# First feed-forward product by the 448 queries of a batch, in a fused attention and feed-forward kernel

## The chip, the core and the metric

The kernel runs on one core of a Trainium2 chip. The metric is the device time of one execution in microseconds (us); lower is better. The core has five engines that run their own instruction streams side by side: TensorE (PE, matmuls; its weight loads are listed apart as PEld), VectorE (DVE), ScalarE (ACT), GpSimd (POOL) and SyncE (SP, which here only issues DMA transfers). Matmul results go to PSUM, which has eight banks of 128 partitions x 512 fp32 values; everything else on the chip lives in SBUF.

## The reference

Attention over 8 batches, 8 heads, 576 positions, head size 64, with a block-causal mask of 64 positions, followed by a feed-forward network over all 4,608 tokens. The weights of the network come in fp64.

```python
scores = (1 / 8) * q @ k.T                       # per batch and head
mask = (pos[:, None] // 64) >= (pos[None, :] // 64)
attn = softmax(where(mask, scores, -1e9))
x = (attn @ v).transpose(0, 2, 1, 3).reshape(4608, 512)
h = x @ w_in                                     # 512 -> 2048
g = h / (1 + exp(-h))
out = g @ w_out                                  # 2048 -> 512
```

## The kernel before, in words

**Precision.** A product that must be near fp32 is made of three matmuls of reduced fp32 (fp32r): each factor is split into a rounded part (`hi`) and the rest (`lo`), and hi*hi, hi*lo and lo*hi are summed in PSUM. ScalarE makes the `hi` copies, GpSimd or VectorE the `lo` differences.

**Attention.** The queries 0 to 127 of every batch (the blocks 0 and 1 of 64) see few keys and are done first, by themselves: the names `a` and `b` in the order table are two groups for queries 0 to 63, `c0` to `c3` four groups for queries 64 to 127. What they give is four blocks of 256 tokens of `x` (blocks 0 to 3). The other 448 queries of a batch and head are one unit, `u0` to `u63`: a batch takes eight units, two heads (a pair of units) fill one of the four 128-row chunks of `x`. A unit has ten score matmuls on TensorE (L639; query widths 448, 320, 192, 448 and 64, each once with the hi and once with the lo part of the queries), then VectorE works on the scores in PSUM: maxima (L582), their spreading over rows (L586), and the subtraction of the maximum (`sub`, L682, L685, and L676 for the half-masked squares). ScalarE takes the exponent (L692), GpSimd splits queries and keys and adds the exponents up (L621, L625, L698, L701). For a pair of units follow twenty matmuls with the values (L742), one multiplication by the inverse sums on VectorE (L746), the `hi` copy of the new chunk of `x` on ScalarE (`x_hi`, L763) and the `lo` difference on GpSimd (`x_lo`, L767).

**First product.** The 3,584 tokens of the units are packed into blocks of 256, numbered 4 to 17, whatever their batch. `ffn1(blk, d, f)` (L970 to L981) makes 128 rows of `h` for one block: four chunks of the contraction by three passes, twelve matmuls 128x256 (L981). Two calls (f = 0 and 1) fill one PSUM bank, of which there are two; ScalarE copies it to SBUF (`keep`, L988) and a DMA takes it to a scratch tensor in HBM (`save`). There are 18 x 16 = 288 such calls. A chunk of `x` of one block is one of 16 tiles, which are given out from a free list as blocks fill and come free when a block's last call is made; a pair's 448 queries fall in two or three blocks (`pieces`, L748 to L759), so `x_hi` and `x_lo` are two or three instructions.

**Weights.** The pieces of `w_in`, `w0` to `w15`, are loaded at the start (L443), turned from fp64 into fp32 (`rebias`, `sign`, `bits`), and split. `w_out` follows as `o0` to `o15` (L447; `rebias` L458). Its eight pairs become the factors `t0` to `t7`: sums of quarters on GpSimd (`x`, L556, L558, L560), `hi` on ScalarE (L570) and `lo` on GpSimd (L575), four parts each, numbered 0 to 3.

**Second product.** `i0` to `i71` are items: a quarter of the contraction for one block, read back from HBM, put through silu (L1006), combined and split, and multiplied in seven products instead of eight (L1055). `y0` to `y17` gather the output. The factors t0 to t7 must all be there soon after the first item starts.

**What sets the order.** Nothing on the chip or in a compiler sorts the work: `ORDER` (L62 to L380) is a table of tokens, and each token emits its instructions on the engines that they run on, so every engine's stream stands in the order of the table. `ffn`, `keep` and `save` take the next call off a queue; the calls of the first product are laid between the steps of the attention so that TensorE has work while the other engines prepare the next unit. `warm:N` puts N small matmuls on zeros there (L783) where TensorE has nothing else. The last 43 calls of `ffn` stand after the last unit and ahead of the first matmul of the second product (`i0.prod:0`); t3 to t7 are made beside them.

Of the kernel before, what the change touches and what calls it, by code (L numbers as in the profile page):

```python
# [66 lines left out]
c0.max:0 w1.hi b.turn:1 c0.exp:0 w2.bits:0 w1.lo warm:8 c0.scores:1 w2.bits:2 w9.load w5.rebias b.back:0 ffn w10.load b.back:1
c0.max:1 w2.hi c1.load c0.exp:1 w2.lo b.pv w3.rebias c0.sum ffn all.mask o0.load w7.rebias w3.bits:0 c3.load_v c0.norm b.hi:0
w3.bits:2 b.hi:1 keep b.lo:0 w11.load w3.hi b.lo:1 warm:8 c0.turn:0 w6.rebias w3.lo w4.bits:0 save c3.scores:0 c0.back:0 w4.bits:1
c0.turn:1 o1.rebias w8.rebias c3.max:0 ffn w4.bits:2 c0.back:1 c3.exp:0 w12.load w5.bits:0 c0.pv w5.bits:1 w4.hi c3.scores:1  # L70
c1.load_v c0.hi w5.bits:2 w4.lo ffn c0.lo w13.load w5.hi c3.max:1 o0.rebias w5.lo w9.rebias w6.bits:0 c1.scores:0 c3.exp:1
w6.bits:1 ffn c1.max:0 keep c3.sum c1.exp:0 w6.bits:2 save c3.norm warm:5 c1.scores:1 w14.load w7.bits:0 w6.hi w7.bits:1
w10.rebias w6.lo c3.turn:0 w7.bits:2 c2.load ffn c1.max:1 c3.back:0 w15.load w8.bits:0 c1.exp:1 c3.turn:1 w8.bits:1 ffn c3.back:1
c1.sum w8.bits:2 w7.hi c1.norm keep warm:8 c1.turn:0 w9.bits:0 w8.hi save w9.bits:1 w11.rebias w7.lo w9.bits:2 c3.pv c1.back:0
w10.bits:0 w8.lo w9.hi c1.turn:1 w10.bits:1 w12.rebias ffn c1.back:1 w9.lo w10.bits:2 w13.rebias w11.bits:0 c1.pv keep w11.bits:1
w10.hi save ffn c1.hi c2.load_v w11.bits:2 w10.lo w14.rebias c1.lo w11.hi c2.scores:0 w12.bits:0 w15.rebias w11.lo w12.bits:1 ffn
u0.load c2.max:0 w12.bits:2 c2.exp:0 warm:5 c2.scores:1 w13.bits:0 w12.hi w13.bits:1 keep w12.lo ffn w13.bits:2 save c2.max:1
w13.hi u1.load w14.bits:0 c2.exp:1 w13.lo ffn w14.bits:1 u0.split_hi c2.sum ffn w14.bits:2 c2.norm keep w15.bits:0 w14.hi save
warm:3 c2.turn:0 w15.bits:1 u0.split_k w15.bits:2 ffn c2.back:0 o0.bits:0 w15.hi u0.split_q o0.bits:1 c2.turn:1 keep ffn o0.bits:2
w14.lo c2.back:1 u2.load o1.bits:0 save c2.pv w15.lo all.staged o1.bits:1 o2.load u0.load_v o1.bits:2 ffn c2.hi u2.load_v t0.x:0  # L80
c3.hi u3.load_v c2.lo t0.hi:0 u1.load_v c3.lo u0.scores t0.hi:1 o3.load t0.lo:0 keep u0.max:0 t0.hi:2 t0.lo:1 save u0.max:1 ffn
u1.split_hi u0.max:2 t0.lo:2 ffn u0.gather u1.split_q u0.top u0.spread ffn keep u0.wide u1.split_k save u0.sub:0 ffn u0.sub:2
u0.exp:0 u3.load t0.x:1 u0.sub:1 u0.exp:2 u1.scores t0.x:2 keep u1.max:0 u0.add:0 u0.exp:1 save u1.max:1 o2.rebias ffn u0.add:1
u2.split_hi u1.max:2 ffn u0.sums:0 u1.gather u2.split_q u0.sums:1 o3.rebias u1.top o2.bits:0 ffn u1.spread u2.split_k o2.bits:1
keep u1.wide t0.hi:3 ffn save o2.bits:2 u4.load t0.lo:3 u1.sub:0 t1.hi:0 ffn o4.load u1.sub:2 u1.exp:0 t1.lo:0 keep u1.sub:1
u1.exp:2 save o3.bits:0 u2.scores u1.exp:1 u1.add:0 u2.max:0 u2.max:1 u1.pv u3.split_hi u1.add:1 u2.max:2 u3.split_k u1.sums:0
u2.gather u1.sums:1 u2.top ffn u1.sums_x u4.load_v u2.spread o3.bits:1 u3.split_q u5.load_v u1.sums_g u2.wide ffn o3.bits:2
u1.sums_m u5.load keep u2.sub:0 t1.hi:1 u2.sub:2 save u2.exp:0 ffn o5.load u2.sub:1 u2.exp:2 t1.lo:1 u1.inverse u2.exp:1 u3.scores
keep u2.add:0 u2.sums:0 u3.max:0 save ffn u3.max:1 u2.add:1 u4.split_hi u1.mult t1.x:0 u2.sums:1 ffn u1.x_hi u3.max:2 u1.x_lo
t1.hi:2 ffn u3.gather keep u3.top u4.split_q u3.spread ffn save u3.wide u4.split_k ffn u3.sub:0 keep u3.sub:1 u6.load t1.x:1  # L90
u3.exp:0 u3.sub:2 u3.exp:1 u4.scores t1.x:2 save u3.exp:2 u4.max:0 t1.lo:2 o5.rebias u4.max:1 u3.pv u5.split_hi u3.sums:0 u3.add:0
u4.max:2 o4.rebias u3.add:1 u4.gather o4.bits:0 ffn u6.load_v t1.hi:3 u5.split_k u3.sums:1 u7.load_v u4.top u3.sums_x u4.spread
o4.bits:1 ffn u5.split_q u3.sums_g u4.wide o4.bits:2 keep u3.sums_m ffn u7.load u4.sub:0 t2.hi:0 u4.sub:2 u4.exp:0 save u4.sub:1
u5.scores u4.exp:2 t1.lo:3 keep u5.max:0 u4.exp:1 u5.max:1 save ffn u6.split_hi u4.add:0 u5.max:2 ffn u6.split_k u4.sums:0
u5.gather u3.inverse u5.top ffn u3.mult u6.split_q u5.spread o5.bits:0 u3.x_hi u5.wide u3.x_lo u8.load ffn keep o5.bits:1 save
u5.sub:0 u4.add:1 ffn u5.sub:2 u5.exp:0 t2.lo:0 keep u4.sums:1 u5.exp:2 u5.sub:1 u6.scores save u5.add:0 u6.max:0 u5.exp:1
u6.max:1 u5.pv u7.split_hi u5.add:1 u6.max:2 u7.split_q u5.sums:0 u6.gather u5.sums:1 u6.top ffn u5.sums_x u7.split_k u8.load_v
u6.spread o5.bits:2 u9.load_v u5.sums_g u6.wide ffn t2.hi:1 u9.load u5.sums_m u6.sub:0 keep u6.sub:2 u6.exp:0 save u6.sub:1
u7.scores u6.exp:2 t2.x:0 u7.max:0 u6.exp:1 u7.max:1 ffn u8.split_hi u6.add:0 u6.sums:0 u7.max:2 t2.hi:2 ffn u6.add:1 keep
u5.inverse u7.gather save u8.split_q u6.sums:1 ffn u5.mult u8.split_k u7.top u7.spread ffn u5.x_hi u7.wide u10.load u5.x_lo keep  # L100
u7.sub:0 ffn u7.sub:2 u7.exp:0 save t2.x:1 u7.sub:1 u7.exp:2 u8.scores t2.x:2 keep u8.max:0 u7.exp:1 save u7.add:0 u8.max:1
t2.hi:3 u7.pv u9.split_hi u8.max:2 u7.add:1 u7.sums:0 u9.split_q u8.gather u7.sums:1 u8.top ffn u7.sums_x u10.load_v u8.spread
u9.split_k u11.load_v u7.sums_g u8.wide ffn u8.sub:0 u11.load u7.sums_m u8.sub:2 u8.exp:0 u8.sub:1 u9.scores u8.exp:2 keep
u9.max:0 u8.add:0 u8.exp:1 u7.inverse save ffn u10.split_hi u8.add:1 u9.max:1 ffn u7.mult u10.split_q u9.max:2 u7.x_hi u7.x_lo ffn
u8.sums:0 u9.gather u8.sums:1 keep u9.top u10.split_k ffn u9.spread save u9.wide u12.load t2.lo:2 ffn u9.sub:0 keep u9.sub:2
u9.exp:0 save t2.lo:1 u9.sub:1 u9.exp:2 u10.scores u9.exp:1 u10.max:0 u9.add:0 u10.max:1 u9.pv u11.split_hi u10.max:2 u9.add:1
u9.sums:0 u11.split_q u10.gather u9.sums:1 u10.top ffn u9.sums_x u12.load_v u10.spread u11.split_k u13.load_v u9.sums_g u10.wide
ffn u10.sub:0 keep u13.load u9.sums_m u10.sub:2 u10.exp:0 save u10.sub:1 u11.scores u10.exp:2 u11.max:0 u10.exp:1 u10.add:0
u11.max:1 ffn u12.split_hi u10.add:1 u11.max:2 ffn u12.split_q u10.sums:0 u11.gather u10.sums:1 keep u9.inverse u12.split_k ffn
save u11.top u9.mult u11.spread u9.x_hi u14.load ffn t2.lo:3 u11.wide keep u11.sub:0 u9.x_lo u11.sub:2 save u11.exp:0 ffn  # L110
u11.sub:1 u11.exp:2 u11.add:0 u11.exp:1 u12.scores keep u12.max:0 u11.add:1 save u12.max:1 u11.pv u13.split_hi u12.max:2
u13.split_q u11.sums:0 u12.gather u11.sums:1 u12.top ffn u11.sums_x u13.split_k u14.load_v u12.spread u15.load_v u11.sums_g
u12.wide ffn u15.load u11.sums_m u12.sub:0 u12.sub:2 u12.exp:0 u12.sub:1 u13.scores u12.exp:2 keep u13.max:0 u12.add:0 u12.exp:1
u13.max:1 save ffn u14.split_hi u12.add:1 u13.max:2 ffn u14.split_q u12.sums:0 u13.gather u12.sums:1 u11.inverse u14.split_k ffn
# [1086 lines left out]
```

## Time and profile before

| what | value |
|---|---|
| median of three executions | 1017.56 us (1017.47 to 1017.73) |
| the profiled execution, its own time | 1016.87 us |
| span of that execution in the trace | 1014.8 us |
| mean granted clock of TensorE | 0.999 of full speed |
| early queries and weights, up to the first score matmul of u0 | 0 to 71.45 us |
| units, with the first product between them | 71.45 to 583.4 us |
| rest of the first product, factors t3 to t7 | 583.4 to 645.4 us |
| second product | 645.4 to 1014.8 us |

The profile is that of one execution. Its own time is 2.07 us more than the span between its first and its last instruction. A row of a grouped view reads: line, engine, operation, output <- input, shape, how many; busy time and mean duration of one; idle time of the engine just before, and whose work ended it. Matmuls overlap in TensorE, so their durations (285 ns on the mean at L981) are longer than the distance between two starts; that distance comes from runs of many equal matmuls in the timeline.

### The profile page before, as it was taken

What the parts mean: (1) busy time and instruction counts of PE and PEld (TensorE: products, weight loads), DVE (VectorE), ACT (ScalarE), POOL (GpSimd) and SP (SyncE); (2) the same over time, 40 slices, a digit from 0 to 9 for tenths busy, and PEclk for the clock granted to TensorE, in tenths of its full rate; (3) what the DMA queues carried; (4) which work ended last, traced back from release to release, by engine and by line L of the source; (5) the groups of instructions that cost most, each with busy time, mean ns of one, the idle gap of its engine ahead of it and who ended that gap; (6) DMA issues with size and microseconds to landing.
All of it is one profiled execution on the core that took longest, in us unless ns stands there. A gap on an engine that the chain in (4) does not pass through costs nothing.

```text
span 1014.8 us, 23816 instructions
## 1 busy us (share of the span) xinstructions
PE 1003.3 (99%) x8532; PEld 946.3 (93%) x8532; DVE 763.0 (75%) x1969; ACT 695.8 (69%) x1587; POOL 626.9 (62%) x770
## 2 busy tenths in 40 slices
...
GB/s 355 362 184 199 138 152 156 151 133 145 149 148 148 141 151 150 150 139 144 149 157 143 74 180 198 205 177 136 146 125 125 141 131 130 131 136 130 141 43 42
DMA packets 76535, 155.70 MB, mean 153 GB/s; under 512 B 9344, under 2 KB 17536, under 8 KB 76416
## 3 DMA queue, kind: packets, MB, share of 16 engines
...
## 4 chain that ended last, share of the span: by engine, by line
PE 92%; ACT 3%; DVE 2%; DMA 2%; issue 1%; POOL 1%; SPq 0%; DVEq 0%; POOLq 0%; ACTq 0%
PE h L981 40%; PE S L1055 24%; PE c L1055 10%; PE S L639 9%; PE U L742 8%; DMA wst<-in_moe_w_in_dram 2%; ACT MR L936 1%; PE S L925 1%; PE S L811 0%; DVE h L1026 0%; ACT x L1039 0%; POOL MR L804 0%; PE S L956 0%; DVE S L1026 0%; ACT wi L1039 0%
## 5 line engine op out<-in xcount | busy, mean ns | idle before, releaser
L981 PE MATMUL h<-x,wi 128*128 128x256 f32 x3456 | 434.7, 285 | 0.6 <-ACT x L763 0.5
L981 PEld LDWEIGHTS h<-x,wi 128*128 128x128 f32 x3456 | 418.9, 191 | 4.2 <-issue 0.9
L582 DVE TRANSPOSE_TENSOR_REDUCE Mx<-S 64x4 f32<-64x128 f32 (+4 forms) x384 | 130.3, 401 | 39.3 <-PE S L639 39.3
L692 ACT ACTIVATE p<-T 128x512 f32<-128x512 f32 (+1 forms) x192 | 112.7, 611 | 27.6 <-DVE T L682 22.1
L988 ACT COPY g<-h 128x512 f32<-128x512 f32 x144 | 84.0, 583 | 41.9 <-PE h L981 31.6
L1043 POOL TENSOR_TENSOR wi<-raw,wi 128x512 fp32r<-128x512 f32 (+1 forms) x56 | 56.9, 1017 | 77.7 <-ACT wi L1039 65.8
L1043 POOL TENSOR_TENSOR x<-raw,x 128x512 fp32r<-128x512 f32 (+1 forms) x58 | 58.9, 1017 | 74.1 <-ACT x L1039 60.0
L617 ACT CAST qh<-qk 128x1024 fp32r<-128x1024 f32 x64 | 67.0, 1048 | 46.8 <-POOL pa L698 21.4
L621 POOL TENSOR_TENSOR qh<-qk,qh 64x576 fp32r<-64x576 f32 x64 | 91.5, 1429 | 6.6 <-POOL pa L698 0.9
L625 POOL TENSOR_TENSOR ql<-qk,qh 128x448 fp32r<-128x448 f32 x64 | 73.7, 1151 | 34.0 <-ACT qh L617 31.8
L698 POOL TENSOR_TENSOR pa<-p 128x448 f32<-128x448 f32 x64 | 73.8, 1153 | 33.6 <-ACT p L692 32.3
L639 PE MATMUL S<-qh 128*128 128x448 f32 (+3 forms) x320 | 91.8, 300 | 0.0
L1006 ACT ACTIVATE raw<-raw 128x1024 f32<-128x1024 f32 x72 | 76.4, 1061 | 19.8 <-DMA raw<-gd 19.4
L742 PE MATMUL U<-p,v 128*64 128x448 f32 (+3 forms) x640 | 86.5, 417 | 0.0
L639 PE MATMUL S<-ql,qh 128*128 128x448 f32 (+3 forms) x320 | 83.6, 306 | 0.0
L742 PEld LDWEIGHTS U<-p,v 128*64 128x64 f32 x640 | 43.0, 137 | 40.5 <-issue 29.8
L685 DVE TENSOR_TENSOR T<-S,MR 128x384 f32<-128x384 f32 (+2 forms) x192 | 73.5, 407 | 0.0
L639 PEld LDWEIGHTS S<-ql,qh 128*128 128x128 f32 (+1 forms) x320 | 57.0, 178 | 5.2
L586 DVE STREAM_TRANSPOSE MR<-m 128x448 f32<-128x448 f32 x64 | 41.3, 645 | 26.9 <-ACT m L664 26.9
L701 POOL TENSOR_TENSOR pa<-pa,p 128x320 f32<-128x320 f32 x64 | 56.1, 876 | 5.3 <-POOL pa L698 0.3
L639 PEld LDWEIGHTS S<-qh 128*128 128x128 f32 (+1 forms) x320 | 57.2, 179 | 2.0
L1043 POOL TENSOR_TENSOR gc<-raw,gc 128x512 fp32r<-128x512 f32 (+1 forms) x30 | 30.5, 1018 | 44.4 <-ACT gc L1039 41.3
...
## 6 DMA issues: line engine op xcount, KB each, us to landing
gd<-g SPq DMA_DIRECT2D x144, 256.0 KB, 2.7
raw<-gd SPq DMA_DIRECT2D x144, 256.0 KB, 2.9
qk<-in_qk_dram SPq DMA_DIRECT2D x128, 256.0 KB, 3.8
...
```

The source lines that it names most:

```text
L582: nc.vector.tensor_reduce(out=out, in_=in_, axis=AX.X, op=op, apply_transpose=True)
L621: nc.gpsimd.tensor_tensor(out=u.qh[64:, NQ:], in0=u.raw[64:, NQ:], in1=u.qh[64:, NQ:], op=ALU.subtract)
L625: nc.gpsimd.tensor_tensor(out=u.ql, in0=u.raw[:, :NQ], in1=u.qh[:, :NQ], op=ALU.subtract)
L639: nc.tensor.matmul(u.ps(c, w, m), u.kk[:, j * P : j * P + m], qq[:, q0 : q0 + w], start=i == 0, stop=i == 1)
L692: nc.scalar.activation(u.p[:, c:e], u.T[:, c:e], AF.Exp, scale=SCALE)
L698: nc.gpsimd.tensor_tensor(out=u.pa, in0=u.p[:, :NQ], in1=u.p[:, 960 : 960 + NQ], op=ALU.add)
L742: nc.tensor.matmul(U[64 * e : 64 * e + 64, q0 : q0 + w], u.vv[:, e, j], z.p[:, c : c + w], start=n == 0, stop=n == 4)
L981: nc.tensor.matmul(h[:, f, :], wi[wt][:, c, w], x[:, xt, :], start=n == 0, stop=n == 3 * CT - 1)
L988: nc.scalar.copy(g.rearrange("p a f t -> p f a t"), hs.pop((blk, d)).rearrange("p f (a t) -> p f a t", a=2))
L1006: nc.scalar.activation(u.raw, u.raw, AF.Silu)
L1043: e.tensor_tensor(out=u.goal(1, k), in0=u.source(k), in1=u.goal(0, k), op=ALU.subtract)
L1055: nc.tensor.matmul(o, quarter(u.g[a], j)[:, P * e : P * e + P], quarter(turned[d].g[b], TORDER[FACTOR[pr]]), start=u.q == 0 and i % 2 == 0 ...
```

## The change

The calls of the first product for the units' tokens are now by batch: a call's group is the 448 queries of one batch (`("b", b)`), its matmuls are 128x448, and a token `ffn` makes half of the contraction (two chunks by three passes, six matmuls). The early blocks 0 and 1, and 2 and 3, are taken together at 512 tokens, except for the first two of eight steps of blocks 0 and 1 each, which stay at 256 and twelve matmuls a token. One PSUM tile now holds one row group f of 448 or 512 tokens instead of two of 256. There are 320 tokens `ffn` and 160 `keep` and `save`, where there were 288 and 144. The matmuls of the first product were 3,456 of 256; they are 1,536 of 448, 336 of 512 and 96 of 256, together 1,968.

`x` has two halves, one for even and one for odd batches; a pair writes its chunk with one `x_hi` and one `x_lo`. A half is written again two batches on, so the `x_hi` of a pair of batch b + 2 must come after the calls for batch b that read the same half of the contraction. For the batches from 3 on the first `x_hi` of a batch stands right behind the last call that it must wait for. The second product still works on blocks of 256 tokens, so an item's read from HBM is cut where a block crosses a batch (`home`). `ROWS` is False; with it the score matmuls stand in the same order as before. Two buffers of the second product (`slots`) are other tiles of `x`.

`ORDER` is a new table. It has 52 `warm` matmuls instead of 106; of the 106, 29 stood after the first `ffn`, of the 52 none does. Ahead of `u0.scores` stand 24 tokens `ffn` instead of 16; between the last unit's value matmuls and `i0.prod:0` stand 49 instead of 43.

```diff
+def fills():
+    out = [((0,), d, None) for d in range(LAG)]
+    out += [((0, 1), d, f) for d in range(LAG, NSTEP) for f in range(2)]
+    out += [((1,), d, None) for d in range(LAG)]
+    out += [((2, 3), d, f) for d in range(NSTEP) for f in range(2)]
+    out += [(("b", b), d, f) for b in range(B) for d in range(NSTEP) for f in range(2)]
+    return out
...
+def home(blk, d):
...
+    out, n = [], 0
+    while n < TB:
+        b, q = divmod((blk - 4) * TB + n, NQ)
+        w = min(TB - n, NQ - q)
+        out.append((("b", b), q, n, w))
+        n += w
+    return out
...
+    def own(g, c):
+        if (g, c) not in x_full:
+            if g[0] == "b":
+                halves = range(2) if g[1] < 2 else (c // 2,)
+                assert filled.issuperset((z, k) for z in before(g[1]) for k in halves), g
+            x_full[g, c] = 0
+
+    def x_batch(b):
+        half = xbuf[:, 8 * (b % 2) : 8 * (b % 2) + 8].rearrange("p n i t -> p (n i t)")
+        return half[:, : CT * 2 * NQ].rearrange("p (c i t) -> p c i t", c=CT, i=2)
...
         def x_hi(u):
-            for _, x, src in u.pieces():
-                nc.scalar.copy(x[:, 0, :], src)
+            own(("b", u.b), u.h // 2)
+            u.x = x_batch(u.b)[:, u.h // 2]
+            nc.scalar.copy(u.x[:, 0], u.xu)
...
-    def ffn1(blk, d, f):
...
-                nc.tensor.matmul(h[:, f, :], wi[wt][:, c, w], x[:, xt, :], start=n == 0, stop=n == 3 * CT - 1)
...
+    def ffn1(z, half):
+        g, d, f = z
...
+        n = width(g)
+        for c in range(CT) if f is None else (2 * half, 2 * half + 1):
...
+            for k, (wt, xt) in enumerate(((0, 0), (0, 1), (1, 0))):
+                o = h[:, TB * half : TB * half + TB] if f is None else h[:, :n]
...
+                nc.tensor.matmul(o, wi[wt][:, c, w], x_of(g, c, xt), start=c + k == 0, stop=c == CT - 1 and k == 2)
...
             for e in range(2):
-                nc.sync.dma_start(out=u.raw[:, e], in_=g_dram[u.blk][2 * u.q + e].rearrange("p a f t -> p (a f) t"))
+                raw = u.raw[:, e].rearrange("p (f a) t -> p f (a t)", f=2)
+                for g, q, n, w in home(u.blk, 2 * u.q + e):
+                    nc.sync.dma_start(out=raw[:, :, n : n + w], in_=g_dram[g, 2 * u.q + e][:, :, q : q + w])
...
-a.load w0.load w3.load b.load w4.load w7.load a.load_v warm:12 a.scores w1.load a.max:0 a.max:1 w0.rebias w0.sign c0.load a.sub:0
...
+a.load b.load a.load_v w0.load b.load_v warm:10 a.scores w1.load w2.load a.max:0 a.sub:0 warm:3 b.scores c0.load a.max:1 a.sub:1
```

The rows of the following fences are the instructions of one engine in the order in which it takes them: line, operation, output <- inputs, shape; "x2" stands for two in a row. Where a tile's name has a number, it tells one use of the tile from the next.

The first is SP's queue of transfers at the very start. `qk` and `v` are the inputs of the groups a and b, `wst` is the staging tile of a weight piece. Before:

```order
L839 DMA qk_241<-in_qk_dram 128x1024
L839 DMA qk_242<-in_qk_dram 128x1024
L443 DMA wst<-in_moe_w_in_dram 128x2x256 x2
L839 DMA qk_249<-in_qk_dram 128x1024
L839 DMA qk_250<-in_qk_dram 128x1024
L443 DMA wst<-in_moe_w_in_dram 128x2x256 x2
L844 DMA v_257<-in_v_dram 128x512
L844 DMA v_258<-in_v_dram 128x512
L443 DMA wst<-in_moe_w_in_dram 128x2x256
```

And now:

```order
L886 DMA qk_257<-in_qk_dram 128x1024
L886 DMA qk_258<-in_qk_dram 128x1024
L886 DMA qk_261<-in_qk_dram 128x1024
L886 DMA qk_262<-in_qk_dram 128x1024
L891 DMA v_265<-in_v_dram 128x512
L891 DMA v_266<-in_v_dram 128x512
L503 DMA wst<-in_moe_w_in_dram 128x2x256
L891 DMA v_271<-in_v_dram 128x512
L891 DMA v_272<-in_v_dram 128x512
L503 DMA wst<-in_moe_w_in_dram 128x2x256 x2
```

The piece w1, without which no `ffn` can start, is the last row's before, with five pieces of weights ahead of or with it; now it is the second piece of all. The values of group b moved ahead of it.

The second is VectorE in unit 29, one of the steady ones, at the subtraction of the maxima; S are the three score banks of the unit in the order of their numbers, MR the spread maxima, and the last row is the first maximum of the next unit. Before:

```order
L682 TENSOR_TENSOR T<-S_4867,MR 128x448
L685 TENSOR_TENSOR T<-S_4869,MR 128x384
L676 TENSOR_TENSOR T<-S_4869,MR 64x2x64
L685 TENSOR_TENSOR T<-S_4868,MR 128x256
L685 TENSOR_TENSOR T<-S_4868,MR 128x128
L676 TENSOR_TENSOR T<-S_4868,MR 64x2x64
L582 TENSOR_REDUCE Mx<-S_5002 128x14
```

And now:

```order
L745 TENSOR_TENSOR T<-S_4215,MR 128x448
L748 TENSOR_TENSOR T<-S_4216,MR 128x256
L748 TENSOR_TENSOR T<-S_4216,MR 128x128
L739 TENSOR_TENSOR T<-S_4216,MR 64x2x64
L748 TENSOR_TENSOR T<-S_4217,MR 128x384
L739 TENSOR_TENSOR T<-S_4217,MR 64x2x64
L642 TENSOR_REDUCE Mx<-S_4316 128x14
```

The third bank, which was emptied second, is now emptied last.

The third is GpSimd at the factor t3, the first that is made after the last unit; `wraw` holds the two pieces of w_out, `xs` the sums, `tb` the factor. Before:

```order
L575 TENSOR_TENSOR tb<-wraw,tb 128x256
L556 TENSOR_TENSOR xs<-wraw 128x512
L558 TENSOR_TENSOR xs<-wraw,xs 128x256
L560 TENSOR_TENSOR xs<-wraw,xs 128x256
L575 TENSOR_TENSOR tb<-wraw,tb 128x512
L575 TENSOR_TENSOR tb<-xs,tb 128x512 x2
```

And now:

```order
L635 TENSOR_TENSOR tb<-wraw,tb 128x256
L616 TENSOR_TENSOR xs<-wraw 128x512
L618 TENSOR_TENSOR xs<-wraw,xs 128x256
L635 TENSOR_TENSOR tb<-xs,tb 128x512
L620 TENSOR_TENSOR xs<-wraw,xs 128x256
L635 TENSOR_TENSOR tb<-wraw,tb 128x512
L635 TENSOR_TENSOR tb<-xs,tb 128x512
```

The third part of `lo` (2) moved ahead of the last sum, and its second part (1), which reads `wraw` itself, is now behind both.

More of the change, by code (lines that the diff above doesn't have):

```diff
@@ L67 @@
[L67 to L114, printed above, removed]
@@ L236 @@
-u62.sub:1 u63.scores u62.exp:2 keep u63.max:0 u62.add:0 u62.exp:1 u63.max:1 save ffn u62.add:1 u63.max:2 ffn u62.sums:0 u63.gather
-u62.sums:1 u61.inverse ffn keep u63.top u61.mult u63.spread save u61.x_hi ffn u63.wide u61.x_lo u63.sub:0 u63.sub:2 ffn u63.exp:0
-keep u63.sub:1 u63.exp:2 save ffn u63.exp:1 u63.add:0 u63.sums:0 u63.pv u63.add:1 keep save u63.sums:1 u63.sums_x u63.sums_g ffn
-u63.sums_m ffn u63.inverse ffn u63.mult keep u63.x_hi save u63.x_lo all.attended o6.load ffn o7.load ffn keep save ffn o6.rebias
@@ new lines @@
+u6.split_k ffn keep u4.sums:1 save u5.sub:0 ffn u5.sub:1 u8.load u3.x_lo u5.exp:0 u5.sub:2 u5.exp:1 t1.lo:3 u6.scores u5.exp:2
+u6.max:0 keep u5.add:0 u6.max:1 u5.pv save u7.split_hi u6.max:2 u5.add:1 u5.sums:0 u6.gather u7.split_q u5.sums:1 u6.top ffn
+u5.sums_x u8.load_v u6.spread u7.split_k u9.load_v u5.sums_g u6.wide ffn u6.sub:0 u9.load u5.sums_m u6.sub:1 u6.exp:0 u7.scores
+u6.sub:2 u6.exp:1 u6.exp:2 u7.max:0 t1.lo:1 u7.max:1 ffn keep u8.split_hi save u7.max:2 u6.add:0 ffn o5.rebias u5.inverse
@@ new lines @@
+u12.top keep u9.mult u12.spread u11.sums:0 save u13.split_k u11.sums:1 u11.pv u9.x_hi u12.wide u11.sums_x u12.sub:0 u15.load
+u9.x_lo u11.sums_g u12.sub:1 u12.exp:0 u12.sub:2 u11.sums_m u13.scores u12.exp:1 u14.load_v u13.max:0 u12.exp:2 u15.load_v
+u13.max:1 ffn u14.split_hi u12.add:0 u13.max:2 ffn keep u14.split_q u11.inverse u13.gather save ffn u11.mult u12.add:1 u13.top
+u12.sums:0 u13.spread u14.split_k u12.sums:1 ffn keep u13.wide u11.x_hi save u13.sub:0 ffn u16.load u11.x_lo u13.sub:1 u13.exp:0
@@ new lines @@
+u40.add:1 save u41.sub:1 u41.exp:0 u42.scores u41.sub:2 u41.exp:1 u39.sums_m u41.exp:2 u40.sums:1 u42.max:0 ffn u43.split_hi
+u42.max:1 u41.add:0 ffn u42.max:2 keep save u43.split_q u39.inverse u42.gather ffn keep u42.top u41.add:1 u39.mult u42.spread
+u41.pv save u41.sums:0 u43.split_k u41.sums:1 u39.x_hi u42.wide u41.sums_x u42.sub:0 u45.load u39.x_lo u41.sums_g u42.sub:1
+u42.exp:0 u43.scores u44.load_v u42.sub:2 u41.sums_m u42.exp:1 u45.load_v u43.max:0 u42.exp:2 ffn u43.max:1 u44.split_hi u42.add:0
@@ new lines @@
+u56.max:2 keep u57.split_q save u53.mult u56.gather ffn u55.sums:0 u53.x_hi u55.sums:1 u57.split_k u55.pv u56.top u55.sums_x
+u56.spread u55.sums_g u59.load u56.wide u53.x_lo keep u56.sub:0 u55.sums_m u56.sub:1 save u56.exp:0 u57.scores u58.load_v
+u56.sub:2 u56.exp:1 u59.load_v u57.max:0 u56.exp:2 ffn u57.max:1 u58.split_hi u56.add:0 u57.max:2 ffn u58.split_q u55.inverse
+u57.gather ffn u56.add:1 keep u57.top u55.mult u57.spread save u56.sums:0 u58.split_k ffn u57.wide u55.x_hi u56.sums:1 ffn
@@ new lines @@
+u59.sub:0 u62.load keep u59.sub:1 u59.exp:0 save u60.scores u59.sub:2 u59.exp:1 u60.max:0 u59.exp:2 u60.max:1 u59.pv u59.add:0
+u61.split_hi u60.max:2 u61.split_q u59.sums:0 u60.gather u60.top ffn u59.add:1 u62.load_v u60.spread u63.load_v u61.split_k
+u59.sums:1 ffn keep u60.wide u57.x_hi save u59.sums_x u60.sub:0 ffn u63.load u59.sums_g u57.x_lo u60.sub:2 u60.exp:0 u60.sub:1
+u60.exp:2 u61.scores u59.sums_m keep u61.max:0 u60.exp:1 save u61.max:1 ffn u62.split_hi u59.inverse u60.add:0 ffn u61.max:2
```

692 lines of the change are left out of this document (364 added, 328 removed).

## The prediction

> **What bounds the kernel now.** I read the page's head first: the span, the busy times and the shares of the chain that ended last.
>
> ```profile
> span 1014.8 us, 23816 instructions
> PE 1003.3 (99%) x8532; PEld 946.3 (93%) x8532; DVE 763.0 (75%) x1969; ACT 695.8 (69%) x1587; POOL 626.9 (62%) x770
> PE 92%; ACT 3%; DVE 2%; DMA 2%; issue 1%; POOL 1%; SPq 0%; DVEq 0%; POOLq 0%; ACTq 0%
> ```
>
> TensorE is busy 99% and carries 92% of the chain. So time comes off only where TensorE gets less to do, and only as far as the others keep up. To see how near they are I asked for windows: a pair of units, the units as a whole, the stretch between the last unit and the second product, and the first items. The columns are busy time (instructions) of PE, PEld, DVE, ACT, POOL, then the granted clock, the DMA share and GB/s.
>
> ```profile
> 302.86:318.64 15.78, 15.78 (x126) 14.23 (x125) 13.42 (x41) 11.21 (x29) 12.21 (x17) 1.00 0.57 158
> 82.00:560.00 478.00, 477.40 (x3751) 430.43 (x3751) 410.06 (x1215) 341.49 (x887) 376.01 (x511) 1.00 0.51 148
> 584.00:645.40 61.40, 61.40 (x514) 61.40 (x514) 22.28 (x33) 34.41 (x60) 40.16 (x43) 1.00 0.62 200
> ```
>
> In the units TensorE never pauses: a pair takes 15.78 us, and VectorE, next in load, works 13.42 of it (85%). The 61.4 us behind the units are TensorE alone.
>
> **The matmuls.** What a matmul costs is the distance between starts. The first row is a piece of the chain, in which 472 equal ones follow each other; the others are one unit's scores in the timeline (start, modelled duration).
>
> ```profile
> 583.43 56.75 PE h L981 x472
> 302.25 0.36 PE L639 MATMUL S<-qh 128*128 128x448 f32 x1
> 302.46 0.36 PE L639 MATMUL S<-ql,qh 128*128 128x448 f32 x1
> 302.66 0.30 PE L639 MATMUL S<-qh 128*128 128x320 f32 x1
> 302.80 0.31 PE L639 MATMUL S<-ql,qh 128*128 128x320 f32 x1
> 302.95 0.25 PE L639 MATMUL S<-qh 128*128 128x192 f32 x1
> 303.04 0.28 PE L639 MATMUL S<-ql,qh 128*128 128x192 f32 x1
> 303.15 0.39 PE L639 MATMUL S<-qh 128*128 128x448 f32 x1
> 303.66 7.44 PE L981 MATMUL h<-x,wi 128*128 128x256 f32 x60
> ```
>
> 56.75 us by 472 is 120.2 ns at 256 columns. At 448 columns the next start comes after 0.20 to 0.21 us, at 320 after 0.14 to 0.15, at 192 after 0.09 to 0.11: from 192 to 448 some 0.105 us for 256 columns, 0.41 ns a column. That leaves about 14 ns of each 256-wide matmul which don't go with its width. The columns are the same before and after (3456 x 256 = 1536 x 448 + 336 x 512 + 96 x 256 = 884,736), so the change saves 3456 - 1968 = 1488 of these 14 ns: 20.8 us. The whole unit, 2,944 columns in ten matmuls, takes 1.41 us (302.25 to 303.66): less 0.41 x 2.944 = 1.21, 20 ns a matmul. If the wide ones cost such 20 ns and those of 256 only 14, the gain is 3456 x 14 - 1968 x 20 = 9 us. The row nearest to the new work is a 448 behind a 448 (0.20 to 0.21, so 16 to 26 ns by the rounding of the trace, at 0.41); yet short matmuls stand in that group, where weights have less time to load. At 15.5 ns for the wide ones, just under that row's low end, it is 3456 x 14 - 1968 x 15.5 = 17.9: I take **-18 us**, ends -9 and -22.
>
> The Trainium skill ("TensorE: Matmul & The Clock Gate", section "Back-to-back issue gap") gives a lone gap of N/2.4 + 2.5 ns, but says that streams of weight load and matmul sustain about 131 ns at 512 columns. By the 131 ns, put to all 1,968 matmuls, the first product would take some 258 us (an estimate from that page) instead of 415; the 0.20 us at 448 in the rows above contradict it.
>
> **The start.** These rows are the landing of w1 (chain), the first `ffn`, the `warm` matmuls after it, and the first score of u0 (timeline of PE).
>
> ```profile
> 7.67 10.07 DMA wst<-in_moe_w_in_dram
> 25.41 1.69 PE L981 MATMUL h<-x,wi 128*128 128x256 f32 x12
> 29.75 1.15 PE L783 MATMUL h<-zero 128*64 128x64 f32 x16
> 40.91 0.80 PE L783 MATMUL h<-zero 128*64 128x64 f32 x10
> 46.96 1.15 PE L783 MATMUL h<-zero 128*64 128x64 f32 x16
> 57.71 0.80 PE L783 MATMUL h<-zero 128*64 128x64 f32 x10
> 64.27 0.56 PE L783 MATMUL h<-zero 128*64 128x64 f32 x6
> 24.39 1.09 PE L925 MATMUL S<-qk 64*64 64x128 f32 x16 [0.47 <-ACT MR L936]
> 71.45 0.44 PE L639 MATMUL S<-qh 128*128 128x448 f32 x1
> ```
>
> The warm matmuls after the first `ffn` (1.15 + 0.80 + 1.15 + 0.80 + 0.56) go: **-4.5 us**, if `ffn` calls fill the places; eight more of those stand there. If not, the place becomes idle time and nothing is won.
>
> w1 lands at 17.74. In the queue before, four `qk` (128x1024 in fp32, 0.52 MB), two `v` (0.26 MB) and five weight pieces (128x512 in fp64, 0.52 MB) come to 5.2 MB up to and with it; now it is the second piece, and they are 4.2 MB. At the mean rate of the start (5.2 MB in 17 us) that is 3.3 us earlier, of which the steps between w1 and the first `ffn` (25.41) hold back some: **-2.9 us** for the first `ffn`, ends 0 and -4. `c0.scores:1` (1.09 us) used to run ahead of the first `ffn` and now runs behind: **+1.05**. TensorE waits at such steps are short today (0.47 us in that row). The groups c1 to c3 still go through ScalarE and VectorE step by step, with idle PE between; where 24 calls don't fit into the holes that 16 and the warms filled, time is lost: **+1.5**, ends 0 and +4. u0's first score comes later in any case, since eight more calls are done by then: 48 x 0.120 + 120 x 0.228 = 33.1 us of them against 192 x 0.120 = 23.1, so 71.45 + 10.0 - 4.5 - 2.9 + 1.05 + 1.5 = 76.6 us (75 to 81).
>
> **The units.** Between u0's first score and u63's values stand 246 calls. A pair has two units of scores (2 x 1.41), the value matmuls (2.63 us by the row below), and about eight calls of 6 x 0.202 = 1.21: 15.15 us where it was 15.78.
>
> ```profile
> 580.79 2.63 PE U L742 x20
> 316.80 0.55 DVE L685 TENSOR_TENSOR T<-S,MR 128x384 f32<-128x384 f32 x1
> 317.46 0.61 DVE L685 TENSOR_TENSOR T<-S,MR 128x256 f32<-128x256 f32 x2
> 306.01 0.20 DVE L733 RECIPROCAL rr<-rs 128x14 f32<-128x14 f32 x1
> 306.25 0.65 DVE L586 STREAM_TRANSPOSE MR<-rr 128x448 f32<-128x448 f32 x1
> 306.94 0.61 DVE L746 TENSOR_TENSOR xu<-U,MR 128x448 f32<-128x448 f32 x1
> DVE Mx L582 <- PE S L639: 39.3, 63, 1.2
> DVE MR L586 <- ACT m L664: 26.9, 59, 0.9
> ```
>
> VectorE's 13.42 us must go into 15.15 (89%). Most of its waits are for scores (39.3 us over 32 pairs, 1.2 a pair), which TensorE makes when the order gets to them and so earlier in a shorter pair; the wait for ScalarE's spreading (26.9, 0.84 a pair) stays. 13.42 + 0.84 = 14.3: it fits. The new order of `sub` empties the second bank ahead of the third, 0.66 us earlier (317.46 less 316.80), and the next unit writes its scores' third part there: no cost, and a little room. What may cost is `x_hi`: at five places (the first pairs of batches 3 to 7) ScalarE waits at it for a call that TensorE has only just got, with `exp` and `keep` queued behind, for which VectorE, GpSimd and TensorE wait in turn. A wait as long as one call is 1.2 us, of which the pair's slack takes most: **+2**, ends 0 and +16 (32 pairs x 0.5, if the fit is missed by half a microsecond).
>
> **Between the products.** From timelines: SP's load of o6 and o7, ScalarE's `rebias` of the first of them, GpSimd's first sums of t3 and of t4, the first item's last `lo` differences, and its first matmul.
>
> ```profile
> 587.60 2.26 SPq L447 DMA_DIRECT2D wst<-in_moe_w_out_dram  x2
> 592.73 0.68 ACT L458 ACTIVATE wraw<-wst 128x512 f32<-128x512 f32 x1 [2.68 <-DMA wst<-in_moe_w_out_dram]
> 597.91 1.30 POOL L556 TENSOR_TENSOR xs<-wraw 128x512 f32<-128x512 f32 x1 [1.08 <-DVE wraw L491]
> 607.48 1.30 POOL L556 TENSOR_TENSOR xs<-wraw 128x512 f32<-128x512 f32 x1 [1.14 <-DVE wraw L491]
> 643.76 2.00 POOL L1043 TENSOR_TENSOR gc<-raw,gc 128x512 fp32r<-128x512 f32 x2
> 645.38 1.60 PE L1055 MATMUL S<-ta,gc 128*128 128x256 f32 x12
> ```
>
> The five factors follow each other on one `wraw`, 9.57 us each (597.91 to 607.48), and the first item's `lo` stands behind t7 on GpSimd. So from the load at 587.60 to the first item's matmul at 645.38 runs a chain of 57.8 us, whatever TensorE does, 62.0 us behind the end of the values at 583.42. Today 43 calls and little else fill these 62 us of TensorE (61.40 of 61.40 in the window above). Now 49 half calls of 6 x 0.202 fill 59.4. The chain: loads issued about 0.4 us earlier by the order, the new row order of t3 up to 1.3 longer, o9 and o13 turned ahead of their mates with 0.6 either way, and up to 1.3 less at its end, where t7's last steps stand in another order: 60 to 62.5. A stall of 0.6 to 3: **+1.5**, ends 0 and +4. Behind it TensorE's work is the same. Sixteen more `keep` in all and item loads in two pieces lie beside a TensorE that is full, and ScalarE is at 69%: 0; if a load were late, each such wait would cost the first items up to 2 us, which the ends above hold.
>
> **Sum.** -18 - 4.5 - 2.9 + 1.05 + 1.5 + 2 + 1.5 = -19.35 us on the profiled execution's 1016.87 (span 1014.8 and 2.07 around it): 997.5. The median of the runs is 0.69 above that execution, so 998.2; I say **998.5 us**.
>
> **Rivals.**
>
> Half bound elsewhere: VectorE with ScalarE's stops, and the factors, take back 7 to 14 us (a pair at 15.3 to 15.5, and a stall of 4): 1005 to 1013. For it speaks that 13.42 of 15.15 us leaves VectorE 1.7 us a pair for all waits, against 2.36 now. Chance 0.15.
>
> Slower: the ring of scores, maxima, subtraction and next scores binds at more than today's period. In odd units the new order puts the inverse, its spreading and the multiplication (0.20 + 0.65 + 0.61 us, rows at 306 above) between the maxima and `top`, on the way to `sub`. At a period p the time is 998.2 + 32 (p - 15.15); it decides from p = 15.82 on (1019.6), and at 15.9 gives **1022 us**. Against it: VectorE's waits for scores, 1.2 us a pair, are there to be used. Chance 0.08.
>
> Width gains nothing: the 14 ns are paid per 256 columns, 448 costs 0.210 us. Then the -18 falls away: 1016.5. The rows show 0.20 or 0.21. Chance 0.05.
>
> No fixed cost once matmuls are wide: the 14 ns are a weight load that outlasts 256 columns and is hidden behind 448. Then a 448 costs 188 ns (0.42 each) and a 512 215: 1536 x 0.013 + 336 x 0.013 = 24 us less, of which 4 come back as a longer stall ahead of the first item: 978. VectorE would still fit (2.82 + 2.63 + 48 x 0.188 = 14.5). Against it: no 448 in the rows starts its follower before 0.20. Chance 0.04. The Trainium skill's lone gap ("TensorE: Matmul & The Clock Gate", "Back-to-back issue gap"), 189 ns at 448, would be this case.
>
> **How the numbers follow.** Forecast 0.68, with the terms' ends 989 to 1006; together with the half-bound case the range is 989 to 1012 and leaves out the cases slower, nothing gained and no fixed cost (0.17) and the tails of the others. A measurement of this kernel can tell about 0.2%, 2 us, from no change. Faster 0.68 + 0.15 + 0.04 = 0.87; same 0.05; slower 0.08.
>
> **What would show it.** Right: runs of 448-wide matmuls with starts 0.20 us apart, in the stretch behind the units; u0's first score at 75 to 81; a pair at 15.0 to 15.3 us with TensorE busy throughout; a hole of PE under 4 us ahead of the first item. Wrong: idle PE in the pair's window with scores waiting on VectorE; a start distance of 0.21 or more; or a PE hole ahead of u0.

## The result

The changed kernel takes 999.86 us (median of four runs, 998.70 to 1000.34) where the kernel before takes 1017.64: a ratio of 0.9822, interval 0.9805 to 0.9839. The same kernel again, later and with its own runs of before, gave 0.9820 (0.9806 to 0.9833). Forecast were 998.5 us, 989 to 1012, and faster with a chance of 0.87.

The profile's head after the change (own time 999.48 us):

```profile
span 997.8 us, 20716 instructions
PE 987.2 (99%) x6936; PEld 888.9 (89%) x6936; DVE 768.4 (77%) x1969; ACT 692.4 (69%) x1555; POOL 616.0 (62%) x722
```

TensorE is still the bound; 16 us of its busy time are gone. Windows by stage show where. After the change the cuts are u0's first score, the end of the last values and the first item's matmul:

```profile
0.00:76.03 76.03, 71.56 (x832) 59.38 (x833) 53.85 (x89) 55.14 (x146) 47.31 (x50) 1.00 0.88 312
76.03:567.05 491.02, 491.02 (x2781) 411.32 (x2779) 436.33 (x1288) 360.00 (x899) 384.19 (x487) 1.00 0.52 149
567.05:626.73 59.68, 59.68 (x298) 55.32 (x295) 22.80 (x36) 33.69 (x63) 38.62 (x42) 1.00 0.62 197
626.73:997.80 371.07, 364.93 (x3031) 362.90 (x3029) 255.40 (x558) 243.52 (x448) 145.90 (x145) 1.00 0.44 127
```

The same stages before:

```profile
0.00:71.45 71.45, 66.38 (x965) 60.34 (x965) 53.22 (x89) 51.28 (x140) 43.27 (x46) 1.00 0.83 297
71.45:583.42 511.97, 511.37 (x4019) 461.21 (x4017) 435.77 (x1290) 364.65 (x943) 398.44 (x539) 1.00 0.51 148
583.42:645.38 61.96, 61.96 (x518) 61.96 (x518) 22.28 (x33) 34.38 (x60) 40.59 (x45) 1.00 0.61 198
645.38:1014.80 369.42, 363.64 (x3038) 362.81 (x3036) 251.70 (x558) 245.51 (x446) 144.58 (x143) 1.00 0.40 126
```

The first column behind the window is its length. Start +4.58 us (with eight more calls done in it), units -20.95, between the products -2.28, second product +1.65: -17.0 us of span. In the units and between the products TensorE has no idle moment: 491.02 of 491.02 and 59.68 of 59.68.

The rows that carry the steps, from TensorE's timeline: the first `ffn`, a run of 512-wide matmuls and the score behind it, a pair of units, and the run behind the last unit with the first item's matmul.

```profile
22.71 1.67 PE L1031 MATMUL h<-x,wi 128*128 128x256 f32 x12
76.03 0.37 PE L702 MATMUL S<-qh 128*128 128x448 f32 x1
77.45 5.74 PE L1031 MATMUL h<-x,wi 128*128 128x512 f32 x24
83.02 0.37 PE L702 MATMUL S<-qh 128*128 128x448 f32 x1
...
287.42 0.36 PE L702 MATMUL S<-qh 128*128 128x448 f32 x1
288.92 2.70 PE L805 MATMUL U<-p,v 128*64 128x448 f32 x20
291.55 3.97 PE L1031 MATMUL h<-x,wi 128*128 128x448 f32 x18
295.37 0.37 PE L702 MATMUL S<-qh 128*128 128x448 f32 x1
296.79 6.32 PE L1031 MATMUL h<-x,wi 128*128 128x448 f32 x30
302.94 0.36 PE L702 MATMUL S<-qh 128*128 128x448 f32 x1
...
567.05 59.84 PE L1031 MATMUL h<-x,wi 128*128 128x448 f32 x294
626.73 1.71 PE L1108 MATMUL S<-ta,gc 128*128 128x256 f32 x12
```

From 567.05 to 626.73 lie 294 matmuls: 203.0 ns each at 448 columns. 24 of 512 take 77.45 to 83.02, 232 ns each with the change to the scores. A pair goes from 287.42 to 302.94, 15.52 us, where it took 15.78.

### The profile page after: what moved, and what is told of

Its sections match the earlier page's. It is cut to its first block, busy times and chain, and to the rows that moved or that the text cites. A ratio compares the mean times of both kernels' runs of the same rounds, so it can differ in the third digit from the quotient of the medians.

```text
span 997.8 us, 20716 instructions
## 1 busy us (share of the span) xinstructions
PE 987.2 (99%) x6936; PEld 888.9 (89%) x6936; DVE 768.4 (77%) x1969; ACT 692.4 (69%) x1555; POOL 616.0 (62%) x722
## 5 line engine op out<-in xcount | busy, mean ns | idle before, releaser
L1031 PE MATMUL h<-x,wi 128*128 128x448 f32 (+2 forms) x1968 | 422.4, 370 | 0.3 <-POOL wi L563 0.3
L1031 PEld LDWEIGHTS h<-x,wi 128*128 128x128 f32 x1968 | 357.3, 188 | 37.4 <-issue 0.9
L1037 ACT COPY g<-h 128x448 f32<-128x448 f32 (+1 forms) x160 | 86.4, 540 | 50.9 <-PE h L1031 36.0
L727 ACT COPY m<-m 32x14 f32<-32x14 f32 x192 | 38.7, 202 | 20.1 <-DVE m L723 18.0
```

The costliest lines, as they stand in the source:

```text
L1031: nc.tensor.matmul(o, wi[wt][:, c, w], x_of(g, c, xt), start=c + k == 0, stop=c == CT - 1 and k == 2)
L1037: nc.scalar.copy(g, hs.pop(z)[:, :n])
```

## The experiments

The theory after the result: TensorE is the bound throughout; a matmul costs a fixed part and a part by its columns, and the change saves 1,488 fixed parts and fills waits of the start with calls. The rivals were a cost by columns alone (the gain then being the new order's), a start whose gain comes from the loads, and a ring around VectorE that was already near its limit.

**What a narrower matmul costs (e1_split).** The same kernel, each wide matmul in two:

```diff
-                nc.tensor.matmul(o, wi[wt][:, c, w], x_of(g, c, xt), start=c + k == 0, stop=c == CT - 1 and k == 2)
...
+                    parts = [(o[:, :TB], x[:, :TB]), (o[:, TB:], x[:, TB:])]
...
+                    parts = [(o[:, i], x[:, i]) for i in range(2)]
+                for i, (oi, xi) in enumerate(parts):
+                    nc.tensor.matmul(oi, wi[wt][:, c, w], xi, start=c + k + i == 0, stop=c == CT - 1 and k == 2, skip_group_check=True)
```

> The changed kernel with each 448-wide matmul of the first product cut into 256 and 192 columns and each 512-wide one into two of 256; the order of everything else stays. 1,872 matmuls are added, no column. Theory (a fixed cost for every matmul, about 10 ns by the changed kernel's trace, where 256 columns take 120.2 ns and 448 take 203.0, so 9.8 ns and 0.431 ns a column; TensorE full): + 18 us, 1018 us, near the kernel before. With the prediction's 14 ns: +26, 1026. Rival (the cost is per column only, and the gain of the change is that of its new order): 1000 us. Rival (a short matmul must wait for the next weights): 192 columns take clearly more than 93 ns, and the time goes over 1030 us.

Measured: 1040.04 us, ratio 1.0217 (1.0202 to 1.0233), 40 us over the changed kernel. The timeline of TensorE in the units, and behind the last one:

```profile
575.62 7.12 PE L1039 MATMUL h<-x,wi 128*128 128x256 f32 x60
582.57 0.39 PE L702 MATMUL S<-qh 128*128 128x448 f32 x1
...
603.45 67.86 PE L1039 MATMUL h<-x,wi 128*128 128x256 f32 x588
671.15 1.62 PE L1116 MATMUL S<-ta,gc 128*128 128x256 f32 x12
```

Thirty pieces of 256 and thirty of 192 take 6.95 us, 231.7 ns a couple; less 120.2 for the 256, a 192 costs 111.5 ns and not 93. That run is short and holds the change to the scores; the 294 couples behind the last unit take 67.70 us, 230.3 ns each, which leaves 110.1 for a 192. So the number of matmuls does matter, but my 18 us were less than half of the 40: the last rival is in it, a short matmul is paced by something else than its columns.

**The cost by width (e11_width).** The last batch's calls, which run behind the last unit with nothing else on TensorE, in two overlapping matmuls of a width that grows with d:

```diff
+                m = 224 + 32 * d
+                parts = [(o, x)] if g != ("b", B - 1) or d == NSTEP - 1 else [(o[:, :m], x[:, :m]), (o[:, NQ - m :], x[:, NQ - m :])]
```

> The changed kernel, where each matmul of the last batch's calls is replaced by two that overlap: of 224 columns in step d = 0, 256 in d = 1, 288, 320, 352, 384 and 416 in d = 6, one of 448 as before in d = 7. The overlapping columns are summed twice, so the sums of that batch are other numbers. They stand in one row behind the last unit, 24 matmul pairs for each step (f = 0 and 1), and the distances of starts give the cost by width. Theory A (weights are loaded at a pace of about 111 ns and hide behind wide matmuls, and beside that there is a fixed 10 ns and 0.431 ns a column): 224 at 111, 256 at 120, 320 at 148, 384 at 175, 448 at 203. Theory B (no fixed cost, 0.453 ns a column from 256 on): 320 at 145, 384 at 174. Theory C (2.4 columns a ns and 14 to 16 ns fixed at all widths): 224 at 108, 320 at 148, 384 at 175. A and C differ at 224 alone.

Measured (one run, 1012.73 us): the matmuls merge into one row, but a ScalarE `keep` follows each row group, that is 12 single matmuls or 24 in couples, so its starts count them. From ScalarE's timeline: a `keep` of the batch before, the last one behind single matmuls (the fourth after it), and from there on every second one, the end of each width:

```profile
579.36 0.53 ACT L1041 COPY g<-h 128x448 f32<-128x448 f32 x1 [1.60 <-issue]
...
589.08 0.54 ACT L1041 COPY g<-h 128x448 f32<-128x448 f32 x1 [0.29 <-PE h L1035]
...
594.43 0.54 ACT L1041 COPY g<-h 128x448 f32<-128x448 f32 x1 [1.63 <-issue]
...
600.20 0.54 ACT L1041 COPY g<-h 128x448 f32<-128x448 f32 x1 [1.97 <-PE h L1035]
...
606.60 0.53 ACT L1041 COPY g<-h 128x448 f32<-128x448 f32 x1 [2.15 <-issue]
...
613.64 0.53 ACT L1041 COPY g<-h 128x448 f32<-128x448 f32 x1 [2.69 <-PE h L1035]
...
621.39 0.54 ACT L1041 COPY g<-h 128x448 f32<-128x448 f32 x1 [2.83 <-issue]
...
629.72 0.53 ACT L1041 COPY g<-h 128x448 f32<-128x448 f32 x1 [2.85 <-issue]
...
638.74 0.54 ACT L1041 COPY g<-h 128x448 f32<-128x448 f32 x1 [1.10 <-issue]
```

The first distance holds 48 single matmuls of 448: 9.72 us, 202.5 ns. Each next one holds the 48 of one width: 224 columns 111.5 ns, 256 120.2, 288 133.3, 320 146.7, 352 161.5, 384 173.5, 416 187.9. From 256 to 448 that is 0.429 ns a column and 10.5 ns fixed, and the widths between lie within 2 ns of this line; 224 lies 5 ns above it, at the 110 to 112 of a 192. Theory A fits. B would have 256 at 116. C would have 224 at 108, and 80 ns between 256 and 448, where the long runs give 120.2 and 203.0. That the floor is the weight load is not shown by these runs; the Trainium skill ("TensorE: Matmul & The Clock Gate", section "LDWEIGHTS (loading the stationary operand)") gives P/1.2 ns for a load of P columns, so 107 ns for 128 (an estimate from that page), and the 111 lies close to it.

**The warm matmuls (e3_nowarm, e2_warm).** Taken out of the kernel before at all five places (the first pair of lines has one of them), and put into the changed one at five (the second pair); the lines are pieces of the order table:

```diff
-w11.load w3.hi b.lo:1 warm:8 c0.turn:0
+w11.load w3.hi b.lo:1 c0.turn:0
...
-c3.max:0 w5.hi ffn save
+c3.max:0 w5.hi warm:8 ffn save
```

> The kernel before without the 29 warm matmuls that stand after the first call of ffn (4.46 us in its trace). Theory (TensorE has nothing else to do at those places: the calls that follow wait for steps of other engines that come no earlier): 0 to -1.5 us, 1016 to 1017.6; the change's gain there came from calls of ffn that fill the places. Rival (the warm matmuls held up what followed them): -3 to -4.5 us, 1013 to 1014.6.

> The changed kernel with 29 warm matmuls put back after the first calls of ffn (8, 5, 8, 5 and 3, each ahead of a call). Theory (TensorE is full from the first call on, and the 4.5 us that such matmuls took were a loss): +3.5 to +4.5 us, 1003.5 to 1004.5. Rival (they fell into waits for the steps of the early groups, and the prediction's -4.5 was not theirs): 1000 us, no difference.

Measured: without them the kernel before takes 1018.67 us, 1.0007 (0.9998 to 1.0016): nothing. With them the changed one takes 1003.50, 0.9851 (0.9834 to 0.9867) against its 0.9822: +3.6 us. First `ffn` and first score of u0, of the one and of the other:

```profile
27.61 1.70 PE L981 MATMUL h<-x,wi 128*128 128x256 f32 x12
73.57 0.44 PE L639 MATMUL S<-qh 128*128 128x448 f32 x1
```

```profile
23.68 1.67 PE L1031 MATMUL h<-x,wi 128*128 128x256 f32 x12
80.92 0.37 PE L702 MATMUL S<-qh 128*128 128x448 f32 x1
```

From call to score: 45.96 us without warms where it was 46.04 with them, and 57.24 us with them where it was 53.32 without. Both theories hold. The warm matmuls lay in waits; what the change did is to put calls there, after which the warm matmuls would cost most of their time (3.6 of 4.46 us).

**The loads at the start (e4_w1, e10_loads).** In the kernel before, w1 moved to second place, and then the changed kernel's order of loads with the old order of steps:

```diff
-a.load w0.load w3.load b.load w4.load w7.load a.load_v warm:12 a.scores w1.load
+a.load w0.load w1.load w3.load b.load w4.load w7.load a.load_v warm:12 a.scores
...
+a.load b.load a.load_v w0.load w1.load w3.load w4.load w7.load warm:12 a.scores
```

> The kernel before with w1 loaded second, right behind w0, instead of fifth of the weight pieces; nothing else is moved. Theory (the first call of ffn waits for w1's landing, 17.73 us in the trace): w1 lands at about 13 us or earlier, the first call starts 1 to 3 us earlier, and 1 to 2.9 us of it stay at the end: 1014.7 to 1016.6. Rival (the first call waits as much for the groups a and b): the first call starts no earlier, 1017.6.

> The kernel before with the transfers at the start in nearly the order of the changed kernel: the inputs of a and b first, then the values of a, then w0, w1, w3, w4, w7; nothing else is moved. Theory (the first call of ffn needs the inputs of b as much as w1, since the steps of b stand ahead of it on TensorE; here both are in the first 3.7 MB): the first call starts at 22.5 to 24 us, and 1.5 to 3 us of it stay at the end: 1015 to 1016.5. Rival (neither sets the start of the first call, but the steps of the other engines): 25 to 28 us, no difference.

Measured: 1019.13 us, 1.0010 (1.0000 to 1.0019), and 1021.63 us, 1.0035 (1.0022 to 1.0049). Both theories fail: the first call came at 28.80 and at 30.10 us, later and not earlier (25.41 in before's profile, 25.75 in e9_pieces' and 27.61 in e3_nowarm's, which start like before). For e4_w1 this is what the rival said, no earlier start and no gain; for e10_loads it is later than the rival's 25 to 28 too. The chain of waits of e4_w1, and below it that of e10_loads:

```profile
3.86 10.44 DMA qk<-in_qk_dram
14.34 1.13 PE S L859 x32
```

```profile
5.13 9.63 DMA wst<-in_moe_w_in_dram
14.84 0.96 POOL wi L468
15.79 0.53 issue
16.33 1.26 POOL wi L503
17.59 1.87 POOL p L804
19.50 1.12 PE S L811 x4
```

In the first the inputs of b come later by the piece that was put ahead, and TensorE's scores of b, in front of the first call, wait for them. In the second GpSimd waits for w3, whose sign step (L468) stands ahead of the normalisation of a (L804) in its stream. So no load sets the start alone: what each engine's next instruction reads must come in the order of all the streams. The changed kernel moved loads and steps together, and its first call came at 22.71 us (22.8 to 24.2 in the eight other profiles of its table and variants). Which part of this the loads have and which the steps, no run tells apart.

**How near VectorE is (e6_dve1, e7_dve2).** One more spreading of the maxima in every odd unit, and in every unit:

```diff
             u.mb = MR[:, :NQ]
             bcast(u.mb, u.m, NQB)
+            bcast(u.mb, u.m, NQB)
```

> The changed kernel with the spreading of the maxima done twice in every odd unit: 0.65 us more of VectorE a pair, on the way from the scores to the subtraction. A pair takes 15.52 us in the changed kernel, with 13.53 us of VectorE. Theory (VectorE has room, TensorE sets the pace): 0 to +1 us, 1000 to 1001. Rival (the ring of scores, maxima and subtraction is near its limit): +0.3 to +0.65 us for each of 32 pairs, +10 to +20 us.

> The same in every unit: 1.3 us more of VectorE a pair, 14.8 of 15.5. Theory: with the waits for ScalarE's spreading (about 0.4 a pair left) 15.2 of 15.5, so it still just fits or costs up to +5 us, 1000 to 1005. Rival (near its limit): +20 us and more.

Measured: 1003.21 us (0.9853, 0.9839 to 0.9868) and 1017.03 us (0.9991, 0.9982 to 1.0000), +3.3 and +17 over the changed kernel. VectorE's waits for scores (Mx) and for ScalarE's spreading (MR) in the units (100 to 560 us), in the changed kernel, in e6_dve1 and in e7_dve2, where none for scores is listed:

```profile
DVE Mx L642 <- PE S L702: 14.8, 30, 1.1
DVE MR L646 <- ACT m L727: 12.2, 23, 0.8
```

```profile
DVE MR L646 <- ACT m L727: 12.0, 23, 0.7
...
DVE Mx L642 <- PE S L702: 2.4, 8, 0.6
```

```profile
DVE MR L646 <- ACT m L727: 11.2, 22, 0.7
```

The wait for scores is the room that is left: 14.8 us in the changed kernel (0.50 a pair), 2.4 with 0.65 us more a pair, none with 1.3. The first takes 0.10 us a pair in time, a sixth of its price, the second 0.53 of its 1.3. So the room was 0.55 to 0.77 us a pair; by the growth of VectorE's busy time in the units, 17.7 and 36.0 us over 32 pairs, it was 0.45 to 0.60. The forecast was right that VectorE fits; but both my expectations were too low (at most +1 and +5 us), and the rival of the ring was that close.

**The second product (e9_pieces, e5_keep, e12_adds, e13_after).** Every item load of the kernel before in pieces; in the changed kernel three late `keep` (one of the three lines is shown), then all `keep` and first `add` (one line), ahead of what stood before them; and the changed kernel unaltered:

```diff
+                for a in range(2):
+                    nc.sync.dma_start(out=u.raw[:, e, 2 * a : 2 * a + 2], in_=g_dram[u.blk][2 * u.q + e][:, a])
...
-i23.prod:1 i30.silu i29.x:2 i27.lo:1 i29.x:1 i23.prod:2 i29.x:3 i31.load i28.hi:0 i29.x:4 i23.prod:3 y5.keep
+i23.prod:1 y5.keep i30.silu i29.x:2 i27.lo:1 i29.x:1 i23.prod:2 i29.x:3 i31.load i28.hi:0 i29.x:4 i23.prod:3
...
-i15.lo:1 y2.keep i16.x:2 i16.hi:0 i11.prod:2 i16.x:1 i19.load y2.add:0
+y2.keep i15.lo:1 i16.x:2 i16.hi:0 i11.prod:2 y2.add:0 i16.x:1 i19.load
```

> The kernel before with every item load cut into two transfers per step of 128 tokens each, as the changed kernel does where a block crosses a batch, but here for all items. Theory (loads in pieces come later, but all but a few lie beside a full TensorE): 0 to +2 us, 1017.6 to 1019.6, with more wait of silu for its load than the 19.4 us of before. Rival (the pieces alone make the stalls of the second product): three stalls or more of over 0.5 us, over +2 us.

> The changed kernel with y2.keep, y5.keep and y10.keep put right behind the product that they wait for, ahead of the silu and the copies that stood before them. Theory (TensorE's three stalls in the second product, 0.67, 0.61 and 0.88 us in the trace, come from a late keep behind a silu that waits for its load): the three stalls go, -1.5 to -2.2 us, 997.7 to 998.4. Rival (the bank is freed late for another reason, the stalls stay): 999.9.

> The changed kernel with every y keep behind the product that it waits for, and every first y add right behind the next product, ahead of the copies, silu and differences that stood before them. Theory (the stalls of TensorE in the second product, 0.3 to 0.9 us each and 1.6 to 2.2 us together, are waits for this first add): none over 0.3 us is left, 997.7 to 998.6. Rival (they are made by late item loads in another way, and move to another place): 999 to 1000 with as much idle TensorE.

> The changed kernel itself, unaltered, beside the other runs on the same chip: 999 to 1000.5 us, to tell what its own spread is and to compare e12 with.

Measured: e9_pieces 1018.33 us, 1.0005 (0.9995 to 1.0014); e5_keep 999.01, 0.9810 (0.9795 to 0.9824); e12_adds 999.25, 0.9814 (0.9800 to 0.9827); e13_after 999.59, 0.9820 (0.9806 to 0.9833). The intervals of the last three and of the first runs of the change overlap; no gain is shown. One of TensorE's stalls in the changed kernel's timeline, and the same place in e5_keep's:

```profile
691.04 1.70 PE L1108 MATMUL S<-ta,wi 128*128 128x256 f32 x12 [0.42 <-DVE g L1143]
```

```profile
691.07 1.70 PE L1108 MATMUL S<-ta,wi 128*128 128x256 f32 x12 [0.21 <-DVE g L1143]
```

The silu's wait for its load over the whole kernel, in before, in the changed kernel, and in e9_pieces:

```profile
ACT raw L1006 <- DMA raw<-gd: 19.4, 25, 2.2
```

```profile
ACT raw L1059 <- DMA raw<-gdb: 36.4, 26, 3.1
```

```profile
ACT raw L1007 <- DMA raw<-gd: 41.2, 36, 2.8
```

Loads in pieces do come later, and it costs nothing that can be measured. The stalls didn't go when `keep` and `add` were moved: TensorE's waits for VectorE's `g` come to 1.59 us in the changed kernel's profile (0.42, 0.45 and 0.72 in the timeline, less than the expectation of e5_keep has), 1.73 in e13_after's, 1.46 in e5_keep's and 1.75 in e12_adds', partly at other blocks; in before's they are 0.40, in e9_pieces' 1.21. The theories of the late `keep` and of the late `add` fall.

e12_adds' profile, of its slowest execution (1002.61 us), has a longer wait ahead of the first item, in the stretch where its table is that of the changed kernel:

```profile
620.83 9.04 PE L1031 MATMUL h<-x,wi 128*128 128x448 f32 x42 [1.43 <-ACT g L1037]
```

The `keep` that TensorE waits for there stands on ScalarE behind a `rebias` of w_out, which had waited 2.42 us for its load.

## Why the prediction was right, point by point

**The matmuls** were the main term, and the mechanism is shown: from 256 columns on a fixed cost for each (e11_width), so that more of them cost more (e1_split). The size was off. I took 15.5 ns for a wide one, "just under that row's low end", and a slope from rows rounded to 10 ns; measured are 10.5 ns and 0.429 ns a column. 1536 x 203.0 + 336 x 232 + 96 x 120.2 = 401 us against 415, so -14 in place of **-18**. The scores' rows had it: a start distance of 0.20 to 0.21 was 203. The rivals' 188 ns (no fixed cost) and 210 ns (width gains nothing) are both excluded.

**The start.** u0's first score came at 76.03 us, forecast 76.6; less the 10.5 us that the eight more calls take (at 232 ns), the start gave -5.9 in place of the -4.85 of its terms. The warm matmuls' -4.5 under its condition, that calls fill the places, held (e3_nowarm, e2_warm). The -2.9 came out at -2.7 (25.41 to 22.71), but not by its reason: w1's landing stands on the chain of before's profile, yet w1 moved ahead by itself brings no earlier call (e4_w1, e10_loads), since other waits then end last. That the number fitted is luck in part.

**The units.** The pair of 15.15 us was a wrong sum: it left out what every change between streams costs. By the same sum the old pair is 5.45 + 84 x 0.120 = 15.55, and it takes 15.78; the new one takes 15.52, outside the 15.0 to 15.3 that I gave as a sign of being right. In the rows above the 30 matmuls take 6.15 us, where 30 x 203.0 ns are 6.09, the 18 take 3.82 instead of 3.65, and the scores ahead of the values 1.50 instead of 1.41. That number didn't enter the total, only the rival's price; and 15.52 doesn't speak for the half-bound rival, since 0.65 us more of VectorE costs only 0.10 (e6_dve1). VectorE fitted, as forecast, with 0.45 to 0.77 us a pair to spare; no idle TensorE shows at `x_hi`, so the +2 is 0.

**Between the products** the 49 half calls took 59.68 us and covered the chain to the end: no stall, where +1.5 was forecast. The chain was not 60 to 62.5 us long behind the last values but at most 59.7. It is near: in e13_after the first item waited 0.45 us for its `lo`, and in e12_adds the stretch was 61.63 us, with the wait of 1.43 shown above. So the 0 of the result's own profile is a good case.

**The second product** took 1.65 us more, where 0 was forecast. Five profiles with the old table take 369.4 to 370.3 us for it, nine with the new one 368.9 to 371.2; the shortest two are e1_split and e11_width, where it starts 15 us later or more. The ranges overlap, so a lasting loss is not shown. What made the 1.65 stays open, since neither pieces nor the places of `keep` and `add` account for it.

In all, against the forecast: matmuls 4 us worse, second product 1.65 worse, start 1 better, `x_hi` 2 and the stall 1.5 better. That is 1.1 us more than the 997.5 forecast for the profiled execution; it took 999.48. The other 0.9 us lie in the units, as far as the windows show: by width their calls cost 22.1 us less (2,736 at 120.2 ns against 48 at 120.2, 216 at 232 and 1,236 at 203.0), and the stage is 20.95 shorter, which fits the dearer changes between streams. So the total came nearer than its terms: errors of 6.5 us one way and 4.5 the other largely cancel, and that is luck.
